# Sort matrices of the first batch by a chain over 64 partitions, the head restaged in the order of the loads, one first layer done ahead

## The chip, the cores and the metric

The kernel runs on one core of a Trainium2 chip. The metric is the device time of one execution in microseconds (us); less is better. Five engines work side by side, each on its own list of instructions: TensorE (PE in the profile, its weight loads PEld), VectorE (DVE), ScalarE (ACT), GpSimd (POOL) and SyncE (SP), which issues transfers.

## What is computed

An attention layer whose blocks of keys and values are first mixed by a small sort matrix, then a dense mixture of four experts (shapes: q, k, v 4 x 8 x 768 x 64, 8 blocks of 96 rows; 3072 tokens, width 512, hidden width 1024).

```
P = sort_net                                   # (4, 8, 8, 8)
for _ in range(5):
    P = exp(P - max(P, -1))
    P = P / (sum(P, -1) + 1e-9)
    P = P / (sum(P, -2) + 1e-9)
k_sorted = einsum('bhij,bhjcd->bhicd', P, k_blocks); v_sorted likewise
attn = softmax(scale * q_block @ k_sorted_block.T)      # inside each block
x    = (attn @ v_sorted), heads side by side             # (3072, 512)
p    = domain_probs / (sum(domain_probs, -1) + 1e-9)
out  = sum over e of p[:, e] * (relu(x @ w1[e]) @ w2[e])
```

## The kernel before, in words

**Tiling.** There are four batches of 768 tokens, each cut into three chunks of 256 tokens. Attention goes by quads of heads (`qd` 0 and 1) in batch 0, by pairs of heads (`pr`) after it. Weights and the natural q, k, v are loaded by GpSimd's queue, which casts them to 16 bits; SyncE's queue does the rest. All is on a manual schedule: each engine executes its instructions in the order in which the source emits them, and a tile framework adds the waits. PSUM is two pools of two buffers each, `psM` and `psA` (tiles of two banks): the third tile of a pool waits until the first has been read.

**Sort matrices.** Before, `sn` (L76) holds all 32 matrices on 32 partitions. Five rounds (L272 to 288) do exp on ScalarE and five or six small operations on VectorE, for all batches at once; `sn16`, `r_half` and `Rs` spread the result over the 128 partitions, and `build_PI0` or `build_PI` multiply it with a mask into the mixing weights. 84 matmuls on constants (`warm`, L249) run beside that.

**The head (L1218 on) and batch 0.** `mix_half` mixes k or v of a quad for one half of the blocks (hf), `mixed` copies it out of PSUM, `h_s` makes scores and their exp, `h_w` transposes mixed v, `h_a` makes attention times v and normalizes it on VectorE (L566, L567), `h_x` transposes the result and copies it into `xT`. `h_k` and `h_v` are mixing and copy in one, `h_q` transposes queries. A query group `qq` is 192 tokens. `group0(qq, nq, g, kcs)` is one eighth of expert 0's first layer for 192 tokens (a quarter of the hidden width for 384); in the head it is emitted in two halves of the width 512 (`kcs` [0, 1] and [2, 3]), between steps of the attention. `second_layer0(hf, slot)` is expert 0's second layer for three columns of 128 tokens; each column's result is read from `psM` by VectorE (L705) into `oacc` or `room`. It calls `slot` twice a column, and the list `later` hands out the rest of batch 0's attention there.

**The other experts.** `chunk_first(b, c, es, first, slot)` does first layers for a chunk, two groups of 16 matmuls each for an expert; VectorE evacuates with relu and the token's weight `pb` (L774). `h_sums` and `weight_sums` (L727 to 745) make the sums that a seven-product scheme for the second layer needs. `chunk` does the rest of a chunk. `PLANS` says in which slot of a chunk which step of the next batch's attention is emitted. Around the change the order is: `second_layer0(0)`, `chunk_first(0, 0, [1, 2])`, the sums of experts 1 and 2, `first_layer0(2, 2)` (32 matmuls of 384 columns, evacuated by ScalarE), `second_layer0(1)`, then `chunk(0, 0)` with expert 3.

Of the kernel before, what the change touches and what calls it, by code (L numbers as in the profile page):

```python
# [17 lines left out]
def kernel(  # L18
# [56 lines left out]
    sn = const.tile([GH, NB, NB], F32, name="sn")  # L75
    nc.sync.dma_start(sn[:], sort_net.rearrange("b h i j -> (b h) i j"))  # L76

# [17 lines left out]
    q0 = Tt[3].rearrange("p a f x -> p (a f x)").rearrange("p (f h r d) -> p f h r d", f=2, h=4, r=R)  # L95

# [34 lines left out]
    def load_w1(e, parts=1):  # L131
        n = NKC // parts
        for i in range(parts):
            nc.gpsimd.dma_start(
                w1sb[e][:, ds(i * n, n)], moe_w1[e].rearrange("(kc p) f -> p kc f", p=P)[:, ds(i * n, n)]
            )
# [4 lines left out]
    def load_half_queries(hf):  # L141
        for qd in range(2):
            nc.gpsimd.dma_start(
                q0[ds(64 * qd, 64), hf].rearrange("p h r d -> p h (r d)"), half_queries(qd, hf)
            )
# [14 lines left out]
    load_half_queries(0)  # L160
# [57 lines left out]

    def spread_weights():
# [13 lines left out]
        pbs[(0, 0)] = load_p(0, 0)  # L233
# [10 lines left out]

    def warm(n):
        ps = psM.tile([P, 4, P], F32, tag="ps", name=f"ps_w_{state['n']}")
        state["n"] += 1
        for m in range(n):
            nc.tensor.matmul(ps[:, m % 4, :], dummy, dummy, start=True, stop=True)  # L249
# [18 lines left out]
    sn16 = const.tile([GH, NB, NB, CP], F16, name="sn16")  # L268
    warm(84)
    p_steps = spread_weights()  # L270
    nc.gpsimd.tensor_copy(ident6, ident[0:R, 0:R])
    for it in range(5):  # L272
        nc.scalar.activation(sn[:], sn[:], AF.Exp, bias=0.0, scale=1.0)
        if it == 4:
            for qd in range(2):
                h_q(qd, 0, nc.scalar.copy)
            warm(30)
        nc.vector.tensor_reduce(srow[:], sn[:], AX.X, ALU.add)
        nc.vector.reciprocal(srow[:], srow[:])
        nc.vector.tensor_tensor(sn[:], sn[:], srow[:].broadcast_to([GH, NB, NB]), ALU.mult)  # L280
        nc.vector.tensor_reduce(scol[:], sn[:].rearrange("p i j -> p j i"), AX.X, ALU.add)
        nc.vector.reciprocal(scol[:], scol[:])
        if it < 4:
            nc.vector.tensor_tensor(
                sn[:], sn[:],
                scol[:].rearrange("p j o -> p o j").broadcast_to([GH, NB, NB]),
                ALU.mult,
            )
            if it:
                next(p_steps)  # L290

    for a, eng in enumerate((nc.vector, nc.gpsimd)):
        eng.tensor_tensor(
            sn16[:, ds(a * HB, HB)],
            sn[:, ds(a * HB, HB)].rearrange("g i (j o) -> g i j o", o=1).broadcast_to([GH, HB, NB, CP]),
            scol[:].rearrange("g j (i o) -> g i j o", i=1).broadcast_to([GH, HB, NB, CP]),
            ALU.mult,
        )

    ps_R = psM.tile([P, 2, 512], F32, tag="ps", name="ps_R")  # L300
    Rv = ps_R[:, :, 0:HB * GH].rearrange("p a (i g) -> p a i g", g=GH)

    def r_half(a):
        for i in range(HB):
            nc.tensor.matmul(
                Rv[:, a, i, :], sn16[:, a * HB + i, :, :].rearrange("g j c -> g (j c)"),
                ident[0:GH, 0:GH], start=True, stop=True,
            )

# [32 lines left out]
    r_half(0)  # L342
    for h0 in range(0, H, 4):
        build_PI0(nc.vector, 0, h0, 4, Rv[:, 0, :, ds(h0, 4)].rearrange("p i g -> p g i"))
# [179 lines left out]
    def side(ps):  # L524

        return ps[:, :, 384:512].bitcast(F16)
# [74 lines left out]
    def st_bk(b, qd):  # L601
# [7 lines left out]
            (1, 0, st_q, 1, 1), (1, 0, st_s, 1, 0), (1, 0, st_n, 1, 2), (1, 1, st_k, 1, 1), (1, 1, st_bv, 2, 0),  # L609
            (1, 2, st_v, 1, 2), (1, 2, st_bk, 2, 0), (1, 2, st_q, 1, 2), (1, 3, st_v, 1, 3), (1, 3, st_n, 1, 3),  # L610
            (1, 4, st_bv, 2, 1), (1, 6, st_a, 1, 0), (1, 7, st_lv, 2, 0),
# [121 lines left out]

    def h_sums(e, which, own=False):
        blk = lambda kh, tok: Hb[:, e, ds(kh * KH, KH), ds(tok * P, P)]
# [23 lines left out]
    def chunk_first(b, c, es, first, slot):  # L759

        xT = xTs[b].rearrange("p k i x -> p k (i x)")
        pb = pbs[(b, c)]
        for e in es:
            for g in range(2):
                ps = psm([P, 4, 2 * P], F32, f"ps_h_{b}_{c}_{e}_{g}")
                for f in range(4):
# [8 lines left out]
                    out=Hb[:, e, ds(4 * g, 4), :], in0=ps[:], scalar=0.0,  # L775
                    op0=ALU.max, in1=pb[:, ds(e, 1), :].broadcast_to([P, 4, 2 * P]), op1=ALU.mult,
# [8 lines left out]
    def chunk(b, c, slot, done=()):  # L785
# [3 lines left out]
        chunk_first(b, c, todo, todo[0], slot)  # L789
# [6 lines left out]
        blk = lambda kh, tok: (lambda e, f: Hb[:, e, kh * KH + f, ds(tok * P, P)])  # L796
# [420 lines left out]

    mk0 = mix_half("k", 0, 0, psm, 8)  # L1218
    mixed("k", 0, mk0, 0, 2, act)
    mv0 = mix_half("v", 0, 0, psa)  # L1220
    mixed("v", 0, mv0, 0, 2, vec)
    h_s(0, 0)
    r_half(1)
    mixed("k", 0, mk0, 2, 2, act)
    vec(Rs.rearrange("p g (a i) -> p a g i", a=2), Rv.rearrange("p a i g -> p a g i"))
    load_half_queries(1)
    load_w2(0)
    build_PI0(nc.gpsimd, 1, 0, H, Rs[:, 0:H, HB:NB])
    h_w(0, vec, 0, 2, tails[("v", 0, 0)])
    mixed("v", 0, mv0, 2, 2, vec)  # L1230
# [3 lines left out]
    ps_a00, ps_s10 = [psa([P, 2, 512], F32, f"ps_{n}") for n in ("a00", "s10")]  # L1234
    h_a(0, 0, ps_a00)
    mv1 = mix_half("v", 1, 0, psm)
    mixed("v", 1, mv1, 0, 2, act)
    h_s(1, 0, ps_s10)
    ps_s01 = psm([P, 2, 512], F32, "ps_s01")
    w01 = h_w(0, None, 2, 2, side(ps_s01))  # L1240
    h_x(0, act, [0], ps_a00)
    h_w(1, vec, 0, 2, tails[("v", 1, 0)])
    mixed("v", 1, mv1, 2, 2, act)
    h_s(0, 1, ps_s01)
    w01(act)
    ps_a10 = psa([P, 2, 512], F32, "ps_a10")
    keep_warm(ps_a10[:, 0, 0:P], 4)
    h_a(1, 0, ps_a10)
    next(p_steps)
    group0(0, 1, 0, [0, 1])  # L1250
    ps_a01 = psa([P, 2, 512], F32, "ps_a01")
    w11 = h_w(1, None, 2, 2, side(ps_a01))
    h_x(0, act, [1], ps_a10)
    h_a(0, 1, ps_a01)
    w11(vec)
    group0(0, 1, 1, [0, 1])
    ps_s11 = psa([P, 2, 512], F32, "ps_s11")
    h_s(1, 1, ps_s11)
    evacuate00 = group0(0, 1, 0, [2, 3], True)
    h_x(1, act, [0], ps_a01)  # L1260
    evacuate00()
    group0(0, 1, 1, [2, 3])
    h_a(1, 1, ps_s11)
    h_k(0, 1, act)
    group0(1, 1, 0, [0, 1])
    h_x(1, vec, [1], ps_s11)
    group0(1, 1, 1, [0, 1])
    h_k(1, 1, vec)
    group0(1, 1, 0, [2, 3])
    group0(1, 1, 1, [2, 3])  # L1270
# [10 lines left out]
    def builds(b):  # L1281
# [8 lines left out]
    builds(1)  # L1290

    later = [
        [(h_q, 1, 1, vec)],
        [(h_v, 1, 1, act)],
        [(h_s, 0, 2)],
        [(h_w, 0, vec), (h_s, 1, 2)],
        [(h_w, 1, act), (h_a, 0, 2)],
        [(h_s, 0, 3), (h_a, 1, 2)],
        [(h_s, 1, 3), (h_a, 0, 3)],
        [(h_x, 2, act), (h_a, 1, 3)],  # L1300
# [3 lines left out]
    def next_stages():  # L1304
        if later:
# [3 lines left out]
    h_v(0, 1, act)  # L1309
    h_q(0, 1, vec)  # L1310
    second_layer0(0, next_stages)
    load_queries(1, range(2))
# [3 lines left out]
    chunk_first(0, 0, [1, 2], 1, next_stages)  # L1316
# [4 lines left out]
    first_layer0(2, 2, next_stages)  # L1321
# [59 lines left out]
```

## Time and profile before

| | us |
|---|---|
| median of 3 runs (lowest, highest) | 362.91 (362.69, 363.76) |
| the profiled execution | 363.03 |
| its span in the trace | 361.3 |
| first half of expert 0's w1 issued, first matmul on it | 6.27, 19.57 |
| first mixing matmul | 12.66 |
| `second_layer0(0)` begins | 28.84 |
| first layer of expert 1 begins | 37.97 |
| `second_layer0(1)`, first to end | 51.90 to 57.08 |

The profile's page gives the busy time of each engine, the span in 40 slices, the transfers, the chain of work that ended last and the costliest groups of instructions. Other views come from the same trace: the chain in order of time, instructions in order of time (start, length, engine, line, operation, output<-inputs, count, and in brackets the idle time before it with what ended it), and busy time in chosen stretches. L705 is line 705 of the kernel. The part of the 363.03 us outside the span is not in the trace.

### The profile page before, as it was taken

To read this page: it belongs to the slowest core of one execution; us is meant where nothing else is said; L and a number is where in the kernel's file an instruction comes from. 1 tells how busy PE (TensorE), PEld (TensorE's weight loads), DVE (VectorE), ACT (ScalarE), POOL (GpSimd) and SP (SyncE) were. 2 spreads that over 40 slices of the span, in tenths; PEclk is the share of its full clock that TensorE was granted. 3 is DMA by queue.
4 is the path that set the end of the run, shared out by engine and by line. 5 is a ranking of instruction groups with operands and counts; after the bars stand their busy time and mean duration, and the time that the engine had idled before them with its cause. 6 is when DMAs were issued, how large, how long until landed. Compare 5 with 4: busy or idle time off the path is not lost.

```text
span 361.3 us, 10846 instructions
## 1 busy us (share of the span) xinstructions
PE 353.7 (98%) x4621; PEld 315.4 (87%) x4621; DVE 276.6 (77%) x561; ACT 173.7 (48%) x306; POOL 134.2 (37%) x148
## 2 busy tenths in 40 slices
PE   8799999999999999999999999999999999999996
PEld 8686867888888888888889999999999998999995
DVE  5654798779788677868878978867679679587694
ACT  2665340451434355368937257175283481571750
POOL 8873010655022330000626318147065082180470
PEclk9999999999999999999999999999999999999999
DMA  7999999999999999935994310110302103102101
GB/s 100 204 206 230 209 210 199 200 192 177 189 167 146 201 121 172 166 80 72 170 200 78 60 60 2 60 60 3 94 27 47 73 3 60 61 2 62 58 11 49
DMA packets 71820, 40.47 MB, mean 112 GB/s; under 512 B 40534, under 2 KB 66524, under 8 KB 71772
## 3 DMA queue, kind: packets, MB, share of 16 engines
q0 software_dynamic: 36560, 19.93, 42.7%
q1 hardware_dynamic: 35068, 19.79, 27.8%
q8 instruction: 36, 0.59, 0.7%
q14 instruction: 12, 0.10, 0.1%
q10 hardware_dynamic: 144, 0.07, 0.1%
HBM read 42.00 MB, written 6.34 MB: 134 GB/s over the span
## 4 chain that ended last, share of the span: by engine, by line
PE 89%; DMA 6%; POOL 1%; DVE 1%; SPq 1%; ACT 1%; issue 1%; DVEq 0%; ACTq 0%; POOLq 0%
PE ps_Q L1141 24%; PE ps_h L768 16%; PE ps_p L753 10%; PE ps_X L1038 10%; PE ps_Z L1038 7%; PE ps_Q L1038 7%; DMA w<-in_moe_w_dram 4%; PE ps_h L661 3%; PE ps_o L696 3%; PE ps_p L803 2%; DMA vs<-arena 2%; PE ps_a L441 2%; PE ps_s L406 1%; PE ps_v L354 1%; SPq L368 1%; PE ps_k L387 1%
## 5 line engine op out<-in xcount | busy, mean ns | idle before, releaser
L1051 POOL TENSOR_TENSOR Hb<-tmp,pb 128x512 f16<-128x512 f32 x40 | 50.8, 1276 | 84.3 <-ACT tmp L1050 83.0
L768 PE MATMUL ps_h<-xT,w 128*128 128x256 f16 x576 | 67.8, 273 | 0.0
L768 PEld LDWEIGHTS <-w 128*128 128x128 f16 x576 | 55.1, 98 | 7.3
L1141 PEld LDWEIGHTS <-Hb 128*128 128x128 f16 x576 | 53.7, 98 | 5.6
L774 DVE SCALAR_TENSOR_TENSOR Hb<-ps_h,pb 128x1024 f16<-128x1024 f32 x36 | 44.0, 1223 | 17.9 <-PE ps_h L768 17.7
L1038 PEld LDWEIGHTS <-w 128*128 128x128 f16 x864 | 52.4, 98 | 1.2 <-issue 0.3
L1141 PE MATMUL ps_Q<-w,Hb 128*128 128x256 f16 (+1 forms) x352 | 43.4, 268 | 0.0
L1038 PEld LDWEIGHTS <-arena 128*128 128x128 f16 x552 | 33.4, 98 | 0.1
L413 ACT ACTIVATE ET<-ps_s 96x768 f16<-96x768 f32 x24 | 18.1, 802 | 26.5 <-PE ps_s L406 26.2
L1038 PE MATMUL ps_X<-kT,arena 128*128 128x128 f16 x384 | 29.3, 219 | 0.0
L1058 ACT COPY ps_X<-ps_Z 128x512 f32<-128x512 f32 x27 | 15.4, 570 | 28.7 <-PE ps_Z L1038 28.3
L396 ACT CAST kT<-ps_k 64x384 f16<-64x384 f32 x48 | 22.7, 474 | 12.8 <-PE ps_k L387 11.8
L1074 DVE TENSOR_TENSOR tmp<-ps_Q,tmp 128x512 f32<-128x512 f32 x26 | 18.0, 692 | 14.1 <-ACT tmp L1073 9.9
L121 POOL DMA_DIRECT2D arena<-in_q_dram x24 | 19.9, 837 | 19.1 <-DMA qT<-arena 18.2
L739 DVE TENSOR_TENSOR Sb<-Hb 128x512 f16<-128x512 f16 x45 | 26.3, 608 | 0.9 <-POOL Hb L1051 0.8
L1141 PE MATMUL ps_Q<-T,Hb 128*128 128x256 f16 x224 | 26.7, 273 | 0.0
L1050 ACT ACTIVATE tmp<-tmp 128x512 f32<-128x512 f32 x40 | 25.4, 634 | 1.2 <-DVE tmp L1074 1.0
L753 PEld LDWEIGHTS <-Hb 128*128 128x128 f16 x232 | 21.9, 98 | 3.0
L1141 PEld LDWEIGHTS <-Sb 128*128 128x128 f16 x240 | 22.1, 98 | 2.3
L1065 ACT COPY tmp<-ps_X 128x512 f32<-128x512 f32 x26 | 15.2, 586 | 13.0 <-PE ps_X L1038 13.0
L1051 POOL TENSOR_TENSOR Hb<-tmp7x,pb 128x512 f16<-128x512 f32 x14 | 19.0, 1355 | 5.7 <-ACT tmp7x L1050 5.7
L1044 DVE SCALAR_TENSOR_TENSOR Hb<-ps_X,pb 128x512 f16<-128x512 f32 x27 | 18.5, 684 | 2.7 <-PE ps_X L1038 2.7
(205 smaller groups left out, 652.8 us busy)
## 6 DMA issues: line engine op xcount, KB each, us to landing
w<-in_moe_w_dram POOLq DMA_DIRECT2D x7, 1024.0 KB, 27.7
pb<-p_dram SPq DMA_DIRECT2D x12, 512.0 KB, 5.5
arena<-in_k_dram POOLq DMA_DIRECT2D x8, 384.0 KB, 9.0
arena<-in_v_dram POOLq DMA_DIRECT2D x8, 384.0 KB, 9.0
vs<-arena SPq DMA_DIRECT2D x36, 66.0 KB, 5.6
arena<-in_q_dram POOLq DMA_DIRECT2D x24, 96.0 KB, 7.5
out_dram<-ob SPq DMA_DIRECT2D x9, 256.0 KB, 2.0
out_dram<-oa SPq DMA_DIRECT2D x8, 256.0 KB, 2.3
```

What stands on the lines that cost most here:

```text
L121: nc.gpsimd.dma_start(t[:, h // 2, :, h % 2, :], q[b, h].rearrange("(t p) d -> p t d", p=P))
L396: nc.scalar.copy(kT[ds(D * hh, D), r], pk[ds(D * r, D), hh].rearrange("p a (i c) -> p a i c", c=CP),)
L413: nc.scalar.activation(ETs[2 * (pr % 2) + hh][:, 0:S].rearrange("c (a x) -> c a x", a=2), pss[hh][0:BLK, :, 0:HS], AF.Exp, bias=0.0, scale ...
L739: tt(sm[0], blk(0, 1), blk(1, 1), ALU.add)
L753: nc.tensor.matmul(ps, lhs(e, f), Ts[e][rhs][:, f, :], start=(first and e == es[0] and f == 0), stop=(done and e == es[-1] and f == KH - 1 ...
L768: nc.tensor.matmul(ps[:, f, :], w1sb[e][:, kc, ds((4 * g + f) * P, P)], xT[:, kc, ds(2 * c * P, 2 * P)], start=(kc == 0), stop=(kc == NKC ...
L774: nc.vector.scalar_tensor_tensor(out=Hb[:, e, ds(4 * g, 4), :], in0=ps[:], scalar=0.0, op0=ALU.max, in1=pb[:, ds(e, 1), :].broadcast_to([P ...
L1038: nc.tensor.matmul(dst[:, ds(f * P, P)], a[lhs][:, k, ds(f * P, P)], t[rhs][:, k, :], start=(first and f == 0 and k == 0), stop=(f == KH - ...
L1044: nc.vector.scalar_tensor_tensor(out=Hb[:, e, ds(i * KH, KH), ds(j * P, P)], in0=src.rearrange("p (f x) -> p f x", f=KH), scalar=0.0, op0= ...
L1050: nc.scalar.activation(src, src, AF.Relu, bias=0.0, scale=1.0)
L1051: nc.gpsimd.tensor_tensor(Hb[:, e, ds(i * KH, KH), ds(j * P, P)], src.rearrange("p (f x) -> p f x", f=KH), pb[:, ds(e, 1), ds(j * P, P)].b ...
L1141: nc.tensor.matmul(ps, lhs(e, f), Ts[e][rhs][:, f, part], start=(first and e == 0 and f == 0), stop=(e == E - 1 and f == KH - 1), skip_gro ...
```

## The change

Four things change.

1. *Batch 0's sort matrices* get a chain of their own, on 64 partitions (head and column), transposed: per round one exp on ScalarE, whose scale is the reciprocal of the last round's sums, one fp32 matmul with a block mask (`blocks8`) that sums over rows, a reciprocal, a product with an accumulated sum, and a reciprocal on VectorE. One fp16 matmul (`sel`, `spread0`) spreads the result over 128 partitions. Two loads (SyncE and ScalarE) bring the matrices; GpSimd makes the mask with a memset and two selects between the first and second query load. 14 warm matmuls stand behind each small one.
2. *The other batches' matrices* keep the old rounds, emitted one step at a time from `next_stages`, that is in the slots of `second_layer0(0)`, of `chunk_first(0, 0, [1])` and of `first_layer0(2, 2)`. `builds(1)` moves there too.
3. *The head* is emitted anew: k0, v0, k1, v1 in turn with all that follows from each, then the whole groups of expert 0's first layer (all of the width 512 at once) with the second halves of mixing and queries between them. w1 of expert 0 is loaded in two halves of its columns, not of its rows. `spread_weights` no longer issues the load of `pb` for chunk 0; that is emitted behind `second_layer0(0)`.
4. *The order after it*: `first_layer0(2, 2)` goes between experts 1 and 2, and expert 1's first layer of chunk (0, 1) is done behind `second_layer0(1)`, into the part of `Hb` that expert 0 has left (`homes`), with its weights in a small load of their own (`pb_1`). `PLANS` for chunk (0, 1) is shifted by two slots.

The core of the diff:

```
+    for n, eng in enumerate((nc.sync, nc.scalar)):
+        eng.dma_start(
+            sn0[ds(32 * n, 32)].rearrange("i (h j) -> i h j", j=NB),
...
     def load_w1(e, parts=1):
-        n = NKC // parts
+        n = FF // parts
         for i in range(parts):
             nc.gpsimd.dma_start(
...
-        pbs[(0, 0)] = load_p(0, 0)
...
+    warm(16)
+    nc.vector.transpose(snT, sn0)
+    now, scale = snT[:, 0:NB], 1.0
     for it in range(5):
+        nc.scalar.activation(e0, now, AF.Exp, bias=0.0, scale=scale)
+        sums = ps_c[0:HJ, 0, ds(it * NB, NB)]
+        nc.tensor.matmul(sums, blocks8, e0, start=True, stop=True)
+        if it < 4:
+            warm(14)
+        else:
             for qd in range(2):
                 h_q(qd, 0, nc.scalar.copy)
+        nc.vector.reciprocal(r0, sums)
+        nc.vector.scalar_tensor_tensor(
+            out=a0, in0=e0, scalar=1.0, op0=ALU.mult, in1=r0, op1=ALU.mult, accum_out=c0
+        )
+        nc.vector.reciprocal(c0r, c0)
+        now, scale = a0, c0r
...
+    def later_steps():
+        for it in range(5):
+            nc.scalar.activation(sn[:], sn[:], AF.Exp, bias=0.0, scale=1.0)
+            yield
+            nc.vector.tensor_reduce(srow[:], sn[:], AX.X, ALU.add)
...
+            if it < 4:
+                nc.vector.tensor_tensor(
+                    sn[:], sn[:], scol[:].rearrange("p j o -> p o j").broadcast_to([GH, NB, NB]), ALU.mult,
+                )
+                yield
...
+    h_s(0, 0)
+    build_PI0(nc.gpsimd, 1, 0, H, Rs[:, 0:H, HB:NB])
...
     mv0 = mix_half("v", 0, 0, psa)
     mixed("v", 0, mv0, 0, 2, vec)
+    mixed("v", 0, mv0, 2, 2, act)
+    ps_s01 = psm([P, 2, 512], F32, "ps_s01")
+    h_s(0, 1, ps_s01)
     h_w(0, vec, 0, 2, tails[("v", 0, 0)])
+    w01 = h_w(0, None, 2, 2, side(ps_s01))
+    w01(vec)
+    h_a(0, 0, ps_a00)
     mk1 = mix_half("k", 1, 0, psm)
     mixed("k", 1, mk1, 0, 2, act)
     mixed("k", 1, mk1, 2, 2, act)
+    h_a(0, 1, ps_a01)
+    h_x(0, vec, [0], ps_a00)
+    h_s(1, 0, ps_s10)
+    h_x(1, vec, [0], ps_a01)
+    h_s(1, 1, ps_s11)
+    mv1 = mix_half("v", 1, 0, psa)
     mixed("v", 1, mv1, 0, 2, act)
+    mixed("v", 1, mv1, 2, 2, vec)
+    h_k(0, 1, act)
     h_w(1, vec, 0, 2, tails[("v", 1, 0)])
+    w11 = h_w(1, None, 2, 2, side(ps_s11))
+    w11(vec)
     h_a(1, 0, ps_a10)
+    h_a(1, 1, ps_a11)
     h_x(0, act, [1], ps_a10)
+    group0(0, 1, 0)
+    h_x(1, act, [1], ps_a11)
+    h_v(0, 1, vec)
+    group0(1, 1, 0)
+    h_w(0, vec)
     h_k(1, 1, vec)
+    group0(0, 1, 1)
+    h_v(1, 1, vec)
+    h_q(0, 1, vec)
+    group0(1, 1, 1)
+    h_w(1, vec)
+    h_q(1, 1, vec)
...
     later = [
         [(h_s, 0, 2)],
+        [(h_s, 1, 2)],
+        [(h_a, 0, 2), (h_s, 0, 3)],
+        [(h_a, 1, 2), (h_s, 1, 3)],
+        [(h_x, 2, act), (h_a, 0, 3)],
+        [(h_a, 1, 3)],
         [(h_x, 3, act)],
     ]
     def next_stages():
+        next(others, None)
         if later:
...
     second_layer0(0, next_stages)
+    pbs[(0, 0)] = load_p(0, 0)
+    pb_1 = load_p_one(0, 1, 1)
...
-    chunk_first(0, 0, [1, 2], 1, next_stages)
+    chunk_first(0, 0, [1], 1, next_stages)
+    first_layer0(2, 2, next_stages)
+    chunk_first(0, 0, [2], 1, next_stages)
     h_sums(1, 4)
     for w in range(1, 5):
         h_sums(2, w)
     all_sums(1, nc.vector)
-    first_layer0(2, 2, next_stages)
     sums2 = weight_sums(2, nc.vector)
-    second_layer0(1, lambda: next(sums2, None))
+    second_layer0(1, with_sums)
     sums0 = weight_sums(0, nc.vector)
+    homes[1] = 0
+    chunk_first(0, 1, [1], 1, next_stages, lambda e: pb_1.rearrange("p (o x) -> p o x", o=1))
+    homes.clear()
```

`with_sums` calls `next_stages` and, from its third call on, one step of `sums2`.

## The prediction

> **What bounds the kernel now.** I read first the page's busy shares and the granted clock, then the chain of waits, then busy time in stretches of my choice, then the order of time on VectorE.
>
> The page's first part:
> ```profile
> PE 353.7 (98%) x4621; PEld 315.4 (87%) x4621; DVE 276.6 (77%) x561; ACT 173.7 (48%) x306; POOL 134.2 (37%) x148
> ```
> Busy time by stretch (columns: the stretch, its length, busy us of TensorE, weight loads, VectorE, ScalarE, GpSimd, then clock, DMA share, GB/s):
> ```profile
> 0.00:20.00 20.00, 16.09 (x340) 14.80 (x341) 12.49 (x46) 9.65 (x19) 16.16 (x39) 1.00 1.02 157
> 20.00:28.84 8.84, 8.84 (x198) 8.01 (x197) 3.63 (x7) 5.49 (x9) 7.22 (x8) 1.00 1.25 208
> 28.84:37.95 9.11, 9.07 (x129) 5.18 (x130) 4.72 (x9) 4.07 (x6) 1.59 (x2) 1.00 1.14 231
> 60.57:361.30 300.73, 297.06 (x3768) 271.20 (x3765) 236.84 (x469) 148.13 (x266) 107.01 (x97) 1.00 0.62 96
> ```
> From 20 us on TensorE has no hole worth the name: 3.7 us idle in 341. So only two things move the end: how much useful TensorE work is done before it runs without holes, and any new hole after that.
>
> The chain of waits, head and 63 us:
> ```profile
> 6.27 13.26 DMA w<-in_moe_w_dram
> 19.52 0.05 issue
> 19.57 0.83 PE ps_h L661 x8
> ...
> 63.70 0.68 DVE T L727
> 64.38 0.34 DVE oacc L895
> 64.73 0.04 issue
> 64.77 1.47 PE ps_p L803 x12
> ```
> The head ends when half of the first expert's w1 lands (19.52). At 63.7 the chain passes through VectorE: a weight sum (L727) stands in its queue ahead of the read (L895) that frees a PSUM bank.
>
> VectorE in order of time, behind the second expert's last layer-1 group:
> ```profile
> 46.72 1.22 DVE L774 SCALAR_TENSOR_TENSOR Hb<-ps_h,pb 128x1024 f16<-128x1024 f32 x1 [0.53 <-PE ps_h L768]
> 47.86 0.42 DVE L741 TENSOR_TENSOR Sb<-Sb,Hb 128x512 f16<-128x512 f16 x1
> ...
> 52.50 0.69 DVE L727 TENSOR_TENSOR T<-w,T 128x1024 f16<-128x1024 f16 x1
> 53.11 0.68 DVE L727 TENSOR_TENSOR T<-w 128x1024 f16<-128x1024 f16 x1
> 53.82 0.75 DVE L705 TENSOR_SCALAR room<-ps_o,p_sb 128x512 f32<-128x512 f32 x1
> ```
> From 46.72 to 53.8 VectorE has no pause. It costs nothing, because TensorE meanwhile does first_layer0(2, 2), 32 matmuls of 384 columns (46.5 to 51.9) that ScalarE evacuates.
>
> [...] pb (512 KB, issued on SP at 26.3) takes 11.7 us to land beside the weights.
>
> **The change, part by part.** The profiled execution is 363.03 us, its span 361.3; the median of the runs is 362.91, so I put the sum on the median.
>
> 1. *Sort chain.* Before, a round is 1.76 us (exp starts at 2.52, 4.27, 6.04), five of them and the spread reach the first mixing matmul at 12.66. After, a round is exp, one small fp32 matmul, reciprocal, product, reciprocal, with 14 warm matmuls (82 ns each, 84 took 6.92) behind the small one. Such a matmul is not in the trace; the nearest (fp32, 6x6) took 0.22 us. With rows of 0.19 to 0.26 a round is 1.25 to 1.5; I take 1.42. Five from 3.0, then h_q (0.85), R0 and the builds (0.4 each): mixing starts at 11.1, 1.5 us sooner. That is no gain by itself: v0 lands at 11.8, k1 at 14.1, v1 at 16.1 (issue plus time to landing), and two selects and a memset on GpSimd (0.3 each by the ident rows) now stand ahead of these loads, so add 0.4 (0 to 0.8).
>
> 2. *Head.* All layer-1 work now waits until both halves of the first queries are through. I follow the queues with the row durations. v0 mixed 12.7; its two copies (VectorE 0.56, then ScalarE 0.48) are in series, and h_w waits for both: 14.35; the second h_w waits for the exp (0.81) that shares its PSUM tile: 15.15; evacuation, h_a, and k1's mixing 15.9 to 16.5; normalizing (0.92 each) to 17.85; the two scores of k1 stand on TensorE behind h_x(0), h_x(1), their exps fill ScalarE from 17.65 to 19.35. v1 has landed at 16.5, but its copy stands behind these exps: 19.85, VectorE's half 20.45, h_w 20.9, evacuation 21.4, h_a 21.85, normalize 22.8, h_x 23.15, copy (0.48) 23.7. First layer 1 at t = 23.7 (w1's half, at about 20, no longer binds). Bounds: 20.6, if nothing stands before v1's chain (before, v1's landing at 16.1 to the copy's end took 4.5 net), to 24.5. Work done before t that stood behind 19.57 before: h_x 2 x 0.17, two h_a 0.48, h_w 0.2, h_s 0.28, one h_k 0.5, and the split groups' overhead 0.35, in all 2.15; against it 8 small matmuls for later batches (0.3, from L305: 4 in 0.26). Break-even t = 19.57 + 2.15 - 0.3 = 21.4. Cost 23.7 - 21.4 = +2.3 (-0.8 to +3.1).
>
> 3. *Loads.* pb's 512 KB move from 26 us to about 18, ahead of most of w2 of expert 0 (28.7 before): at most 2.5 us later, 31.5. It is wanted at t + 8.8 = 32.5 (four groups at 1.31, mixes, transposes). Nothing; if t were 20.6 it would cost up to 2. w1 split by columns: nothing. The 3.5 us of layer 1 done ahead is only moved; it leaves later experts' loads more slack than the 1.5 to 3 us that they had.
>
> 4. *Other batches' sort rounds in the second layer.* Each is 1.44 us of VectorE (2.80 to 4.24) plus an exp on ScalarE. second_layer0(0) takes 8.65 us of TensorE; VectorE must now do three oacc (0.75), four normalizes (0.93) and three rounds in it, 10.3 us, beginning 2.5 us late. From its start: oacc 2.65 to 3.4, round 3.4 to 4.9, normalize to 5.8 (h_a(1, 2) wants that PSUM tile at 5.2: wait 0.7), oacc to 6.6, round to 8.05, normalize to 9.0 (h_x(2) wants it at 7.4: 1.7), normalize 10.7, oacc 11.7, round 13.15, normalize 14.1 (h_x(3), behind one layer-1 group, at 12.7: 1.4). +3.8 (1.5 to 4.5). The R matmuls wait for the last spread: +0.3 (0 to 0.6).
>
> 5. *first_layer0(2, 2) moved ahead of expert 2.* second_layer0(1) now follows expert 2's last group directly, so the cover of section one is gone. From that group's end VectorE does the evacuation (to 1.3), seven h_sums (47.86 to 50.33: 2.5) and four weight sums (2.8), and only then the first oacc: 6.6 to 7.4. psM has two buffers: columns 3 and 4 take 1.73 each, column 5 wants column 3's at 3.5. Wait 3.9 (3.4 to 4.1), the surest item. The groups after it wait 0.2 more.
>
> 6. *Next chunk's layer 1 ahead.* 32 matmuls and two evacuations, moved; its chunk has two groups fewer, between which batch 1's attention hides: 0 (-0.5 to +1).
>
> Sum: 2.3 + 3.8 + 0.3 + 3.9 + 0.2 = +10.5, of which I take 10.1 since some lag can overlap: 362.9 + 10.1 = **373.0 us**.
>
> **Rivals.**
> A. Only the wait of step 5 is real; the rounds slip between VectorE's other work and the head is even: +3.9 + 0.3, 367.1. For it: VectorE is only 4.72 of 9.11 us busy in 28.84 to 37.95. Against: the rounds and normalizes are in one queue, in the order above.
> B. The main case, and the clock falls to half after the waits (3.9 us idle at column 5, thin work at 17 to 23): [...] +3.4: 376.4. [...] Against: a clock of 1.00 in a head that is busy 16.09 of 20.
> C. Not slower: what stands ahead in ScalarE's and VectorE's queues is done before it is in the way. Then v1's chain starts at its landing (t = 20.6) and no bank waits: steps 4 and 5 are 0, the head -0.8, 362.1. Place and point: ScalarE's exps must be over by 16.7 (I count 19.35) and VectorE's queue behind expert 2 must be shorter than the 3.5 us that two buffers cover (I count 7.4). For it: TensorE has hardly a hole now. That the shorter sort chain brings no earlier mixed values, since loads gate them, is in all three.
>
> **How the numbers follow.** Main 0.60 (370 to 376 by its own bounds), A 0.21, B 0.10, C 0.09 (0.05 below 361.8, 0.04 between). About 0.3% is what a measurement here tells from no change. Range 366.0 to 376.5: it takes in A about its centre and B's, and leaves out C and the far side of B. Faster 0.05, same 0.04, slower 0.91.
>
> **What would show it.** Right: first layer-1 matmul near 23.7; a wait of TensorE of near 3.9 us before the third column of second_layer0(1), released by VectorE's oacc; waits of 1 to 2 us of h_x(2) and h_x(3) on normalizes; idle TensorE after 24 us near 12 instead of 3.7. Wrong: a first layer-1 matmul before 21.4, columns 3 to 5 back to back, or holes that the rest of the kernel gives back.

## The result and the profile after

The changed kernel takes **381.93 us** (median of 4 runs, 380.78 to 383.77) against 363.27 (median of 4): ratio 1.052 (95% interval 1.047 to 1.057), or **+18.8 us**. The forecast was +10.1. Below, "over before" is each kernel's ratio to the kernel before on the same chip, times 362.9; the ratios leave out executions that took over 1.5% longer than the same kernel's fastest (one each of e1, e6, e9 and e18, two of e3's four, and two of e4's five, with which e4's median would lie 18 us over before), so they can differ from a difference of two medians.

The profiled execution of after took 383.77 us (span 382.1). Its page, part 1 and TensorE's granted clock by slice of 9.55 us:

```profile
PE 362.4 (95%) x4586; PEld 319.8 (84%) x4586; DVE 285.5 (75%) x590; ACT 172.9 (45%) x308; POOL 135.2 (35%) x152
...
PEclk9958999699999999999999999999999999999999
```

TensorE is busy for 8.7 us more (353.7 before) with 35 instructions fewer: matmuls became slower, not more. The last line shows where the clock fell: 5 and 8 in the third and fourth slice, 6 in the eighth. Of the 20.8 us that the span grew, the other 12.1 are waiting. The stretches of after, cut where the prediction cut them (columns: sum; PE, PEld, DVE, ACT, POOL busy; clock; DMA share; GB/s):

```profile
0.00:20.00 20.00, 15.56 (x275) 13.10 (x275) 9.05 (x40) 8.93 (x17) 15.91 (x41) 0.94 1.02 152
20.00:37.48 17.48, 15.97 (x285) 14.44 (x281) 7.62 (x14) 6.18 (x10) 5.24 (x7) 0.67 1.20 218
37.48:47.53 10.05, 8.69 (x102) 4.53 (x98) 7.17 (x24) 4.52 (x8) 1.49 (x2) 1.00 1.20 207
47.53:81.53 34.00, 28.36 (x206) 19.54 (x203) 25.83 (x49) 5.37 (x8) 5.73 (x6) 0.90 0.85 133
81.53:382.00 300.47, 293.82 (x3736) 268.18 (x3733) 235.82 (x467) 147.92 (x266) 106.83 (x97) 1.00 0.56 90
```

The second line is the head's end: 17.5 us where before had 8.8, at a mean clock of 0.67. Half rate lasts from 17.7 to 31.4 us and again from 68.9 to 75.8. TensorE's waits in after, longest first:

```profile
PE ps_o L770 <- DVE room L779: 4.7, 1, 4.7
PE ps_x L654 <- DVE xsl L641: 1.7, 2, 0.9
...
PE ps_s L480 <- DVE Sb L819: 1.0, 1, 1.0
PE ps_h L845 <- DMA xT<-xsl: 0.9, 1, 0.9
```

The first is the wait forecast at column 5, the second the two of h_x(2) and h_x(3) on the normalizes; the last two lie in later chunks, at 106.5 and 138.1 us, where none was forecast. VectorE ahead of column 5, to set against the lines of before from 46.72 to 53.82:

```profile
60.13 1.22 DVE L851 SCALAR_TENSOR_TENSOR Hb<-ps_h,pb 128x1024 f16<-128x1024 f32 x1 [2.12 <-PE ps_h L845]
61.27 0.92 DVE L815 TENSOR_TENSOR Sb<-Hb 128x512 f16<-128x512 f16 x1
62.11 1.21 DVE L851 SCALAR_TENSOR_TENSOR Hb<-ps_h,pb 128x1024 f16<-128x1024 f32 x1
63.24 1.14 DVE L817 TENSOR_TENSOR Sb<-Sb,Hb 128x512 f16<-128x512 f16 x1
64.31 0.41 DVE L819 TENSOR_TENSOR Sb<-Hb 128x512 f16<-128x512 f16 x1
...
68.61 0.69 DVE L801 TENSOR_TENSOR T<-w,T 128x1024 f16<-128x1024 f16 x1
69.22 0.74 DVE L779 TENSOR_SCALAR room<-ps_o,p_sb 128x512 f32<-128x512 f32 x1
```

The queue is the forecast one: evacuation, sums, four weight sums, and only then column 3's evacuation (69.22), for which TensorE has waited since 65.3. New are 0.92 and 1.14 us in place of 0.41 for the first two sums. The head's end on TensorE in after:

```profile
24.86 0.50 PE L654 MATMUL ps_a<-perm,xsl 96*128 96x96 f16 x4 [0.58 <-DVE xsl L641]
25.16 0.52 PE L735 MATMUL ps_h<-xT,w 128*128 128x192 f16 x2
25.93 2.40 PE L735 MATMUL ps_h<-xT,w 128*128 128x192 f16 x14 [0.25 <-ACT xT L658]
28.12 0.53 PE L654 MATMUL ps_a<-perm,xsl 96*128 96x96 f16 x4
```

Layer 1 begins at 25.2 (19.57 before). A group of 16 matmuls of 192 columns takes 2.45 us at half rate (at 29.4) and 1.49 at full rate (at 32.7).

### The profile page after: what moved, and what is told of

Same layout as the page of the kernel before. It is cut to its first block, busy times and chain, and to the rows that moved or that the text cites. A ratio compares the mean times of both kernels' runs of the same rounds, so it can differ in the third digit from the quotient of the medians.

```text
span 382.1 us, 10831 instructions
## 1 busy us (share of the span) xinstructions
PE 362.4 (95%) x4586; PEld 319.8 (84%) x4586; DVE 285.5 (75%) x590; ACT 172.9 (45%) x308; POOL 135.2 (35%) x152
## 5 line engine op out<-in xcount | busy, mean ns | idle before, releaser
L845 PE MATMUL ps_h<-xT,w 128*128 128x256 f16 x576 | 68.8, 275 | 0.9 <-DMA xT<-xsl 0.9
L851 DVE SCALAR_TENSOR_TENSOR Hb<-ps_h,pb 128x1024 f16<-128x1024 f32 x34 | 41.4, 1222 | 18.7 <-PE ps_h L845 16.6
L1151 DVE TENSOR_TENSOR tmp<-ps_Q,tmp 128x512 f32<-128x512 f32 x26 | 18.0, 692 | 14.8 <-ACT tmp L1150 10.6
L142 POOL DMA_DIRECT2D arena<-in_q_dram x24 | 19.8, 836 | 24.2 <-DMA qT<-arena 18.1
L815 DVE TENSOR_TENSOR Sb<-Hb 128x512 f16<-128x512 f16 x45 | 28.1, 648 | 0.0
L1128 POOL TENSOR_TENSOR Hb<-tmp7x,pb 128x512 f16<-128x512 f32 x14 | 18.8, 1345 | 5.5 <-ACT tmp7x L1127 5.5
```

What stands on the lines that cost most here:

```text
L142: nc.gpsimd.dma_start(t[:, h // 2, :, h % 2, :], q[b, h].rearrange("(t p) d -> p t d", p=P))
L815: tt(sm[0], blk(0, 1), blk(1, 1), ALU.add)
L845: nc.tensor.matmul(ps[:, f, :], w1sb[e][:, kc, ds((4 * g + f) * P, P)], xT[:, kc, ds(2 * c * P, 2 * P)], start=(kc == 0), stop=(kc == NKC ...
L851: nc.vector.scalar_tensor_tensor(out=Hb[:, homes.get(e, e), ds(4 * g, 4), :], in0=ps[:], scalar=0.0, op0=ALU.max, in1=weights(e).broadcast ...
L1128: nc.gpsimd.tensor_tensor(Hb[:, e, ds(i * KH, KH), ds(j * P, P)], src.rearrange("p (f x) -> p f x", f=KH), pb[:, ds(e, 1), ds(j * P, P)].b ...
```

## Experiments

### The clock, the moved group and VectorE's queue

**e1, warm head.** Edit (six places in all, 49 matmuls):

```
     h_s(0, 1, ps_s01)
+    ps_a00 = psa([P, 2, 512], F32, "ps_a00")
+    keep_warm(ps_a00[:, 0, 0:P], 12)
...
     h_k(0, 1, act)
+    open_group(0, 0, 10)
```

> The changed kernel with 49 idle-filling 128x128x128 matmuls on TensorE in the gaps of the head (12 and 5 while it waits for the first transposes of v, 6 before the second h_x, 10, 6 and 10 between 21 and 25 us), nothing else. Theory T1 (the clock fell at 17.7 us because the restaged head streams too little through the array, and the half rate to 31.4 us costs time of its own): granted clock 1.00 from 17 to 31 us, the two layer-1 groups of 16 matmuls back at 1.3 us from 2.9 and 2.3, second_layer0(0) begins about 4 us earlier (33.5 instead of 37.5), time 3 to 4.5 us under the changed kernel's 381.9 (378). Rival W (the head's end is set by waits for VectorE, ScalarE and loads, the clock is incidental): clock back to 1.00, but second_layer0(0) within 0.7 us of 37.5, time the same within 1 us.

Measured: +17.6 over before (15.1 to 20.1). Half rate in the head shrinks from 13.7 to 3.4 us, yet layer 1 begins no earlier (25.3) and second_layer0(0) at 35.6 instead of 37.5: 1.9 us, where T1 promised 4 and W under 0.7. In time T1 promised 3 to 4.5 us and W none to 1; 1.2 were measured, with intervals that overlap (17.1 to 20.6 for the changed kernel), so no gain is shown. The fillers may themselves hold TensorE back: ahead of one of them it stood 0.9 us with nothing recorded that it waits for (in e3 ahead of two, 0.8 and 1.2).

**e2, group back.** Edit:

```
-    chunk_first(0, 0, [1], 1, next_stages)
-    first_layer0(2, 2, next_stages)
-    chunk_first(0, 0, [2], 1, next_stages)
+    chunk_first(0, 0, [1, 2], 1, next_stages)
...
     all_sums(1, nc.vector)
+    first_layer0(2, 2, next_stages)
```

> The changed kernel with first_layer0(2, 2) put back behind the sums of experts 1 and 2, as in the kernel before, nothing else. T1 (the wait of 4.7 us at column 5 is VectorE's queue, and the idle time pulls the clock to half for 6.8 us, which costs another 3.4 us): no wait over 1 us at column 5, no half clock at 69 to 76 us, time 7.5 to 8.5 us under the changed kernel (374). Rival W (the wait alone): 4 to 5 us (377.5). Rival Q (VectorE's queue is the bound there whatever the order of TensorE's work, since the sort rounds and sums lie on it): the wait comes back later, under 2 us gained.

Measured: +20.1 (19.2 to 21.0), nothing gained. The column's wait is gone, and this stands in its place, first among e2's waits:

```profile
PE ps_R L377 <- DVE sn L367: 6.0, 2, 4.8
```

The matmuls that transpose the late sort's result (ps_R) now stand on TensorE just behind the sums, and the second half of their input (sn) is queued on VectorE behind eight sums and four weight sums. The clock falls here too, from 62.7 to 69.5 us. Rival Q, with its place named.

**e3, both.**

> Both edits: the warm matmuls in the head and first_layer0(2, 2) behind the sums. T1: clock 1.00 throughout the first 100 us and the sum of the two gains, 11 to 13 us under the changed kernel (370); what is left over the kernel before, some 6 to 7 us, is the later start of the first layer-1 group, the waits for the sort rounds and the waits in the next chunk. Rival W: 5 us (377).

Measured: +19.7 (18.3 to 21.2). The profiled run has clock 1.00 from 7.7 to 62.3 us, so it shows the head without the clock: layer 1 at 25.5, the first column at 35.8. In e2, at half rate from 14.9 to 28.6, the first column is at 36.0, though mixing began 0.8 us earlier there (11.4 and 12.2). From mixing to the first column full clock is thus worth about 1 us in this pair. T1's sum fails.

**e4, the wait at column 5 filled.** Edit: in with_sums, at its fourth call,

```
+        if after["n"] == 4:
+            keep_warm(psa([P, 2, 512], F32, "ps_kw")[:, 0, 0:P], 72)
```

> The changed kernel with 72 idle-filling matmuls into a spare PSUM tile ahead of column 5 of second_layer0(1), while TensorE waits there for VectorE; order and wait unchanged. It tells the price of the clock from that of the wait: T1: the wait (filled) still ends at the same time, but the clock stays 1.00 from 69 to 76 us, and the time falls by 3.0 to 3.6 us (378.5). Rival W (TensorE would wait for VectorE's sums after column 5 anyway, so a slower column costs nothing): under 0.7 us.

Measured: +15.7 (14.5 to 16.9), about 3 us gained in three of five executions. The clock stays at 1.00 there, and the first product begins at 78.7 instead of 81.5. But in the profiled execution (385.9 us, not in the ratio) TensorE then waits 3.0 us at 113 and the clock falls there instead (0.92 over 110.0 to 116.4 us): pb of the third chunk, asked for at 103.1, lands at 115.0. In after it lands at 115.8, just in time. Part of what is gained early can be lost to a transfer.

**e8, group back, with the late sort's last step ahead of the sums.** Edit to e2:

```
+    next(others)
     h_sums(1, 4)
```

> The kernel of e2 (first_layer0(2, 2) behind the sums) with one more step of the other batches' chain ahead of the sums, so that the second half of its result isn't queued behind eight sums and four weight sums on VectorE, where e2 had TensorE wait 4.8 us for it. T2 (in the changed kernel and in e2 the same mechanism, a short VectorE result queued behind expert 2's sums, cost a wait and with it the clock): no wait over 1.5 us between 50 and 75 us, clock 1.00 there, time 7 to 9 us under e2's 383 (375). Rival Q (VectorE is the bound of this stage in any order): a wait of 3 us or more comes up at another place before 85 us, and the time is within 3 us of e2's.

Measured: +16.2 (14.6 to 17.7), 4 us better than e2. The wait for ps_R falls from 4.8 to 2.6 us and half rate from 6.8 to 3.4 us; no other wait over 0.9 comes between 20 and 85 us. T2 in part: the queue's order decides, and the result is still late.

### The parts taken out one by one

**e5, four of five late rounds left out.** Edit in later_steps:

```
     for it in range(5):
+        if it:
+            yield
+            if it < 4:
+                yield
+            continue
```

> The changed kernel with four of the five sort rounds of the other batches left out (their exponentials and their VectorE work; what is read as their result is the first round's), and the order of everything else kept. Theory T1 (the rounds cost only the three waits of h_a and h_x in second_layer0(0), 0.5 + 0.9 + 0.9 us; at column 5 VectorE is late because of expert 2, having idled 2.1 us before it): the three waits fall to under 0.5 us in all, the wait at column 5 stays at 4 to 5 us with its fall of the clock, time 2 to 2.5 us under the changed kernel's 381.9. Rival Q (VectorE has too much to do from 40 to 70 us, whatever the order): the wait at column 5 falls under 2 us too, and the clock stays up: 8 us or more.

Measured: +13.2 (11.6 to 15.0), 5.6 us gained where T1 gave 2 to 2.5. The three waits in second_layer0(0) are gone, as it said; column 5 keeps its 4.8 us, but half rate behind it lasts 3.4 instead of 6.8 us, which is no part of T1 and worth up to 1.7 us of the gain (an estimate: half of the 3.4 us less).

**e6, the head of before.** Edit: the head's steps, load_w1 and the list `later` from the kernel before, without r_half.

> The changed kernel with the head of the kernel before from the end of the sort chain to second_layer0(0): the same order of mixes, scores and split groups, w1 of expert 0 in halves of the contraction, and the old list of later stages; the new sort chain, the late rounds, the moved group and the work done ahead stay. T1 (the restaged head costs some 6 us by itself at full clock and 2 more through the clock): first layer-1 matmul at 19.6, clock 1.00 up to the wait at column 5, second_layer0(0) begins at 29 to 30 instead of 37.5, time 7 to 9 us under the changed kernel (374). Rival S (it is the new chain, its thin warm-up and the late rounds that cost the time): under 3 us gained.

Measured: +15.0 (13.1 to 17.0), about 3.8 gained. Layer 1 begins at 19.4 and the first column at 30.2: up to there the profile gains 7.3 us against after, 5.8 against e2 and e7, whose head is that of after. T1's place is right and its size too large.

**e7, no work ahead** (chunk_first(0, 1, [1], ...), homes and pb_1 out, PLANS of before).

> The changed kernel without the first layer of expert 1 of the next chunk done ahead (and with the plan of slots of the kernel before), nothing else. T1 (the work is only moved, and what it costs are the two waits in the next chunk, 1.0 and 0.9 us, which come from the plan that was shifted for it): time 1 to 2.5 us under the changed kernel. Rival P (the work ahead gives TensorE something to do where VectorE is late, so it pays): 1 us or more above the changed kernel. Rival N: within 0.7 us.

Measured: +16.8 (14.8 to 18.8), 2.0 gained. The two waits of the next chunk are gone (idle from 100 to 210 us: 0.4 instead of 2.1).

**e10, e7 with column 5's wait filled as in e4.**

> The kernel of e7 (no work ahead) with the 72 idle-filling matmuls of e4 ahead of column 5, to price the clock where no later transfer is near: same order, same wait for VectorE. T: clock 1.00 from 30 us on, time 2.8 to 3.4 us under e7's 379.2. Rival W (the half-rate stretch is hidden, since VectorE's weight sums hold the next products anyway): within 0.7 us of e7.

Measured: +16.3 (15.5 to 17.1), within 0.5 us of e7 (14.8 to 18.8): the time that rival W named, but not W's reason. The products did not wait for VectorE's sums: the stretch got shorter, and the first product came at 74.0 instead of 75.8. The same 40 matmuls in e7, and in e10:

```profile
68.50:75.80 7.30, 7.28 (x40) 4.47 (x40) 5.09 (x7) 0.00 (x0) 0.00 (x0) 0.70 0.05 8
```

```profile
68.80:74.00 5.20, 5.17 (x40) 3.88 (x40) 4.92 (x7) 0.00 (x0) 0.00 (x0) 1.00 0.02 5
```

2.1 us less, still 1.4 at 150 us; then TensorE waits 1.3 us at 194 us for a load of values (vs), and the first ps_X matmul begins at 201.9 in both.

**e11, GpSimd's builds four slots later in program order.**

> The kernel of e7 with GpSimd's four builds for the later batches begun four slots later, so that they don't run beside VectorE's first sums of experts 1 and 2. T (those sums took 0.92 and 1.14 instead of 0.41 us because of GpSimd's builds): the two sums take 0.41, the wait at column 5 is 3.4 to 3.7 instead of 4.7 us, time 1.0 to 1.3 us less than e7's 379.2, unless the builds slow VectorE just as much where they are now. Rival I (the sums are slow for another reason): sums and wait unchanged.

Measured: +17.1 (16.0 to 18.1). Nothing moved: the builds still began at 58.4, since nothing stood ahead of them on GpSimd but their input. So this did not test the theory.

**e15, the transposing matmuls five slots later,** so that the builds must be (five `yield` ahead of ps_R in later_steps).

> The kernel of e7 (no work ahead) with the transposing matmuls of the other batches five slots later, so that GpSimd's four builds, which need their result, run after column 5. Theory B (GpSimd's builds beside them slow VectorE's sums): the first two sums take 0.41 instead of 0.92 and 1.14, the wait at column 5 falls from 4.7 to 3.4 to 3.6, the weight sums after it are slowed instead, time 0.5 to 1.3 us under e7's 379.2. Rival I (another reason): sums and wait unchanged.

Measured: +17.5 (16.9 to 18.1). VectorE, then GpSimd in e15:

```profile
59.49 0.42 DVE L820 TENSOR_TENSOR Sb<-Hb 128x512 f16<-128x512 f16 x1
...
63.70 0.68 DVE L806 TENSOR_TENSOR T<-w 128x1024 f16<-128x1024 f16 x1
64.42 1.42 DVE L806 TENSOR_TENSOR w<-w 128x1024 f16<-128x1024 f16 x1
65.87 1.42 DVE L806 TENSOR_TENSOR T<-w 128x1024 f16<-128x1024 f16 x1
```

```profile
64.04 1.25 POOL L414 TENSOR_TENSOR arena<-maskv,Rs 128x512 f16<-128x512 f16 x1 [12.49 <-ACT Rs L385]
...
66.71 1.49 POOL L414 TENSOR_TENSOR arena<-maskv,Rs 128x512 f16<-128x512 f16 x1
```

Theory B's mechanism is shown: with the builds gone from beside them the first sums take 0.42, and the weight sums that now run beside the builds take 1.42 instead of 0.69. They are ahead of column 3's evacuation too, so the wait grew to 5.75 us, and no time was gained.

**e12, the kernel before without its 30 fillers in the fifth sort round** (the line `warm(30)` out).

> The kernel before without the 30 idle-filling matmuls between the fourth and fifth sort round; order, waits and all else as they were. It prices the clock in the head by itself. T [...]: half rate from about 12.2 us, for two to four stretches of 3.4 us, and the first layer-1 groups at half rate; time 1.5 to 4 us over the kernel before. Rival W (in the head the loads bind, w1 landing at 19.5): half rate shows, but time within 0.5 us.

Measured: +1.2 (0.7 to 1.8). Two stretches of it:

```profile
10.90:21.10 10.20, 9.29 (x174) 8.05 (x175) 4.75 (x11) 5.34 (x11) 8.30 (x11) 0.50 1.22 206
21.10:30.40 9.30, 9.25 (x200) 8.31 (x198) 4.75 (x10) 6.22 (x11) 7.36 (x8) 1.00 1.21 211
```

10.2 us at half rate, and the first column comes 1.6 us later (30.4 for 28.8). In this head, which waits for loads and copies, half rate cost about a sixth of its length.

### What is left with the chain alone

**e9, the chain with its late rounds, and nothing else of the change** (e6 and e8 and e7 together, ps_R one slot later).

> The kernel before with nothing but the new sort chain for the first batch and the other batches' rounds done late: the head of before, first_layer0(2, 2) behind the sums, no work ahead, and the other batches' last result taken ahead of the sums with its transposing matmuls one slot later, so that neither queues behind expert 2. Theory T (the losses are separate and add up: restaged head, moved group with its wait and clock, work ahead, late rounds): what is left is the late rounds' two waits of about 0.9 us and one stretch of half clock in the head that cost e6 1.4 us up to second_layer0(0), so 3 to 5 us over the kernel before (366 to 368), no wait over 1.5 us after 30 us. Rival S (the chain and the late rounds cost more than their waits show): 370 or more. Rival G (a shorter chain pays once nothing else is in the way): 362.5 or less.

Measured: +8.7 (7.7 to 9.8): rival S. Nearly half of the change's loss is here. The stretch from the end of second_layer0(0) to the first product takes 27.0 us in e9 and 23.2 in the kernel before. Its lines, of before, then of e9:

```profile
37.40:60.60 23.20, 23.14 (x209) 16.65 (x210) 19.48 (x32) 6.46 (x8) 2.23 (x3) 1.00 1.28 206
```

```profile
42.50:69.50 27.00, 23.48 (x200) 16.26 (x197) 25.66 (x49) 7.19 (x10) 7.42 (x7) 1.00 1.25 196
```

TensorE's work is the same; VectorE goes from 19.5 busy of 23.2 to 25.7 of 27.0, and GpSimd from 2.2 to 7.4. VectorE has become the bound of this stretch, with no half clock in it. Of its 6.2 us more, 3.0 are four weight sums that take 1.42 to 1.54 us beside GpSimd's builds and 0.69 each before; the rest is the rounds. By place, e9's profile loses 3.3 us up to the first column (1.8 of them a wait for w2), 1.8 in second_layer0(0) and 3.8 here, and next to nothing behind it.

**e13, e9 with four of the five late rounds left out.**

> The chain-alone kernel of e9 with four of the five late rounds left out as in e5 (what is read as their result is the first round's). Theory Q2 (the rounds fill VectorE from the end of second_layer0(0) to the products, where e9 has it busy 25.66 of 27.00 us, so that the transposing matmuls' input and the columns come late): the waits of 0.9, 1.1 and 1.8 us after 38 us go, the stretch from the end of second_layer0(0) to the first product falls from 27.0 to 24 or less (before 23.2), time 4 to 5.5 us under e9's 372.2 (367). Rival R (it is the sums slowed beside GpSimd and the place of the result, not the rounds): under 2 us.

Measured: +6.2 (5.4 to 7.0), 2.5 gained; the stretch is 25.2 us. Q2 in direction, half in size: a wait of 1.95 at column 5 stays. VectorE is busy 22.5 us in the stretch, the 19.5 of before and the 3.0 of the slowed weight sums, so both Q2 and rival R had a part.

**e14, e13 with the last step of the probabilities where it was before** (`next(p_steps)` behind h_a(1, 0)).

> The kernel of e13 with the last step of the probabilities back behind h_a(1, 0), as in the kernel before, so that pb's 512 KB are asked for some 6 us later. Theory L (pb ahead of w2 of expert 0 delays it): w2 of expert 0 lands near 29.5 instead of 32, the wait of 1.8 us at the first column goes, time 1.5 to 2 us under e13. Rival: w2 lands when it does for another reason (the queue's own start), within 0.5 us of e13.

Measured: +6.3 (5.3 to 7.3). w2 of expert 0 lands at 29.1 instead of 31.2, and the first product comes 1.6 us earlier (64.3), as theory L says; two waits at 102 and 124 us (1.0 and 1.7) take it back in the profiled run, and the times show no gain.

**e16, the same with all rounds kept.**

> The chain-alone kernel of e9, all rounds kept, with the last step of the probabilities where it was before. Theory L: 1.5 to 2 us under e9's 372.2 (370.4), first column of second_layer0(0) without a wait over 0.5 us. It still computes everything; if theories L and Q2 hold, no order of these parts beats the kernel before, since the rounds' 5 us on VectorE are more than the chain can save.

Measured: +9.3 (7.0 to 11.6). First column at 29.6 instead of 32.0; time unchanged within its interval. The chain of e16 that ends at the third chunk shows where it went in that run:

```profile
116.88 1.60 PE ps_p L830 x15
118.48 10.23 DMA xT<-xsl
128.71 0.04 issue
128.75 1.25 PE ps_h L846 x10
```

A transposing transfer of xT took 10.2 us from its issue; its like before (issued at 111.1, landed at 117.1) took 6.0.

**e17, e14 with the late sort's one round, result and builds ahead of second_layer0(0)** (`for _ in others: pass`).

> The kernel of e14 (four of the five late rounds left out; what is read as their result is the first round's) with the one round, its result, the transposing matmuls and GpSimd's builds ahead of second_layer0(0). Theory B2 (the builds beside VectorE's weight sums, and the place of the result, make the remaining 6 us): no wait at column 5, the stretch from the end of second_layer0(0) to the first product at 23 to 23.5 us as before (25.2 in e14), time 2 to 4 us under e14's 368.5. Rival H (the new chain and its colder TensorE cost it): under 1 us gained.

Measured: +6.9 (5.9 to 7.9). B2 is right on the stretch, 22.5 us with no wait at column 5; but TensorE waits 3.0 us for sn at the new place, at 30 us, half rate follows (clock 0.83 over 30 to 40 us), and no time is gained.

**e18, e16 with all rounds spread over eleven steps of the head** (`next(others)` behind each).

> The kernel of e16 with all rounds kept and spread over the head, one step behind each of eleven head stages, the transposing matmuls and builds in second_layer0(0). Everything is computed. Theory P (the rounds cost what they cost by where they stand on VectorE: in the head it is idle more than half the time, from 42 to 70 us it is full): the stretch from the end of second_layer0(0) to the first product falls from 27 to 23 to 24 us, the head gets 1 to 2 us longer, time 3 to 5 us under e16's 371.4 (367.5), still over the kernel before. Rival: each round delays an evacuation on the head's own chain, which loses as much: within 1.5 us of e16.

Measured: +4.1 (3.0 to 5.2), 5 us better than e16. The stretch of e18:

```profile
41.10:63.70 22.60, 22.59 (x193) 16.20 (x194) 18.59 (x30) 5.65 (x7) 3.67 (x5) 1.00 1.29 205
```

VectorE is back at 18.6 and TensorE without a hole. The first column is at 31.4 (29.6 in e16), the price in the head. The profiled execution took 373.2 us and is not in the ratio: behind this stretch, at 121.7, TensorE waits 4.2 us for a transposing transfer of xT. Theory P, but not alone: the builds moved too, to 36.1 to 40.2 us, where e16 has them at 55.1 to 60.6, and the weight sums are back at 0.69. By VectorE's busy time that is 3.0 of the 7.1 us by which this stretch is lighter than e9's. It is the fastest version of the change with everything computed, and slower than before.

## Why the prediction was wrong

The direction held (0.91 for slower) and the named waits came, but the time lies 5.4 us above the range. The main case's sum is one of waits and of order. It had no term for slower matmuls, and TensorE's busy time grew by 8.7 us; idle TensorE after 24 us came to 14.5 us where 12 was forecast. By stretch of the profiled run, cost against before. What was only moved is taken off: 2.0 us of stages done in the head instead of second_layer0(0), 0.5 us of ps_R matmuls done after it, 1.1 us of attention done in it instead of behind it, 3.5 us of layer 1. The wait of h_x(3) is in the second row, as in step 4.

| stretch | forecast | measured |
|---|---|---|
| to the first column (32.5 forecast, 37.5 measured) | +2.3 | +7.2 |
| second_layer0(0) and h_x(3) | +3.8 | +2.6 |
| to the first product | +4.4 | +7.7 |
| from there to the last matmul, and behind it | 0 | +2.2, +1.1 |
| sum | +10.5 | +20.8 |

**Step 1** (mixing at 11.1; its terms one after another give 11.75): 12.4. The second and third round took 1.9 us each, not 1.42: with 16 warm matmuls before the first round instead of 84, the clock rose at 7.5 us (5.4 before), and until then warm matmuls stood 0.107 us apart instead of 0.056. (The clock of 1.00 in the views counts the time before its first record as full rate.) The step put this at nothing, since loads gate what follows. In the restaged head they do not. The mixing of k0, v0 and v1 in after:

```profile
12.40 0.57 PE L557 MATMUL ps_mk<-Sb,arena 128*64 128x64 f16 x24
13.81 0.57 PE L557 MATMUL ps_mv<-Sb,arena 128*64 128x64 f16 x24
20.04 0.85 PE L557 MATMUL ps_mv<-Sb,arena 128*64 128x64 f16 x24
```

v0 had landed at 12.46 and v1 at 16.76; neither mix waits for its load, each stands behind other work on TensorE. The nine kernels with this head and no fillers in it (after, e2, e4, e5, e7, e8, e10, e11, e15) began mixing anywhere from 11.3 to 12.8 us, early where the clock rose early (4.6 to 9.6 us), and all began layer 1 12.5 to 13.2 us later, where the prediction has 12.6. So the 1.3 us of step 1 go through to layer 1 almost whole. In the head of before the loads do gate: e9, e16, e17 and e18 mix v1 within 0.3 us of its landing.

**Step 2** has the row with the largest miss, but not in its walk from mixing to layer 1: 12.8 us, where 12.6 was forecast. Then the four groups and what stands between them took 12.3 us, not the 8.8 of "t + 8.8". e1 and e3 at full clock took 10.3, so 1.5 of this is more work and copies between the groups than was counted (e3's TensorE waits 0.4 and 0.3 us for xT there), and 2.0 is the clock. With step 1's 1.3 that makes nearly all of the 5 us by which the first column is late. The parts are by place in the traces; as a test, e6 takes the restaged head away and has the first column 5.8 to 7.3 us sooner, which bounds order and clock together, and e12 prices 10.2 us at half rate in the other head at 1.6.

**Step 3** (loads, nothing): right for after, whose late head hides it. Where the head is as before, e13 against e14 shows the 2 us that step 3 named for that case (31.2 against 29.1).

**Step 4** was right on the place and too large on the waits (0.5, 0.9, 0.9, against 0.7, 1.7, 1.4). It missed that the rounds don't end in second_layer0(0): three of them, and the spread, come after it. e5 gains 5.6 us in all; e18 gains some 5 on e16 by moving rounds and builds. The step failed in treating a queue's delay as local.

**Step 5** was right in mechanism: 4.7 against 3.9, released by VectorE's evacuation. The mis-sized term is the sums, 0.92 and 1.14 for 0.42, and e15 shows GpSimd's builds to be the cause. Before, they ran at 23.6 to 27.6 us, in the head; after, at 59.9 to 64.1. Had the step followed GpSimd's queue, it would have seen them move here. What the step put at nothing is the half rate behind the wait, from 70.0 to 75.8: 2.9 us, the amount by which e4's first product comes earlier.

**Step 6** (nothing, -0.5 to +1): e7 puts it at 2.0 us, with an interval as wide as that. The plan of slots was shifted for it and two results came late.

**The clock** was set at 1.00 in the main case on the ground of a head "busy 16.09 of 20". That was the wrong measure (TensorE was busy 2.20 of 3.45 us ahead of the fall at 17.7 in after, and 2.12 of 3.40 in the kernel before where the clock held), and it is the step that failed most: by place it is 2.0 us in the head and 2.9 behind column 5, nearly half of the 10.3 us that the sum was short. Rival B had both places right (17 to 23 us, column 5); its +3.4 was the author's estimate, for half rate that came to last 13.7 and 6.8 us. As a price in time it stays open: e4 got about 3 us back at column 5 in some executions, e10 none that shows, e1 no gain in time that shows, though its first column came 1.9 us sooner. In e4 and e10 the traces show later waits that took the gain back. Of what e9 leaves out (head, moved group, work ahead), 10 us came back together, where e6, e8 and e7 alone gave 3.8, 2.6 and 2.0.

Open: e13 is still 6 us over before with four late rounds gone. By place 2.4 of them lie ahead of the first column (e14 takes 1.6 of these away, with pb's load), 0.9 in second_layer0(0), 2.0 in the stretch behind it, which e17 removes there and loses again in the head, and 0.5 at the end. Why the head of before is still 0.8 us later with the new chain (first column at 29.6 in e14 and e16, 28.8 before), and how often the transfers at 100 to 130 us take a gain back, was not settled.

## What to carry to other kernels

A shorter chain buys nothing where loads gate what follows, and where they do not, each microsecond that it is late goes through. The work put off has to stand somewhere: ask which engine is full there (19.5 of 23.2 us was VectorE's mark here) before asking whether each wait is covered. Follow GpSimd's queue too where its operations come to stand beside VectorE's (1.42 us for 0.69 in e15), and let a result that another engine waits for stand ahead of bulk work. Where a tuned kernel keeps TensorE warm on purpose (e12: 30 fillers fewer, 10.2 us at half rate), count what the array streams in a thinned stage (0.51 against 0.29, the estimate below), not its busy share (2.12 of 3.40 us against 2.20 of 3.45).

## What the hardware showed

**The clock fell where little of the array streamed, with TensorE as busy as where it held.** Between its recorded changes in after the clock keeps one value for 10.24, 13.65, 37.55, 6.83 and 307.2 us, all whole multiples of 3.413 us. A stretch of the kernel before through which it stayed at 1.00, then the stretch of after that ends with the fall at 17.7:

```profile
8.80:12.20 3.40, 2.12 (x38) 1.92 (x38) 2.62 (x11) 1.62 (x3) 2.17 (x12) 1.00 1.26 190
```

```profile
14.20:17.65 3.45, 2.20 (x62) 1.80 (x57) 1.85 (x5) 1.71 (x3) 3.45 (x5) 1.00 1.31 207
```

TensorE is busy for 0.62 and 0.64 of the two, and in after no gap is over 0.9 us. What differs is the matmuls: before, 32 fillers of 128x128x128 and four small transposes; in after, mixes of 64 columns on half of the array and small transposes and scores. Columns streamed, times the share of the array's rows and columns in use, at 0.42 ns a column (24 matmuls of 512 columns took 5.18 us before, from 51.90 to 57.08), come to 0.51 of the stretch before and 0.29 of that in after, each matmul counted where it starts; without the share, to 0.52 and 0.48. This is an estimate from the matmul records of the two traces. e12 leaves out 30 such fillers, and its clock is 0.50 from 10.9 to 21.1 us. Over the first 100 us of after, cut into windows of 3.413 us from the first record of the clock on (7.48), the same sum is 0.40 or more in the windows that kept 1.00, 0.31 and 0 in the two before a fall, 0.21 to 0.41 in those that left the clock at half, and 0.44 and 0.50 in the two that raised it. Where a matmul at an edge is counted moves a window by up to 0.06.

**VectorE's sums on SBUF took twice as long beside GpSimd's builds.** f16 tensor_tensor operations of VectorE on SBUF took 1.42 instead of 0.69 us (128x1024) while GpSimd ran its builds, tensor_tensor on SBUF too (e15; in e9 1.42 to 1.54). GpSimd's own took up to 1.49 us there (e15), and 1.04 to 1.07 in the kernel before (from 23.57). Operations of VectorE that read PSUM kept their time beside the builds: the normalize in the kernel before 0.69 (24.17 us; 0.69 at 21.32, without a build beside it), the evacuations in after (60.13 and 62.11 us) 1.22 and 1.21, against 1.23 with GpSimd idle (78.24 us).
